# A held opening in another order: chunk 3's scores ahead of chunk 2's y, the first weight loaded one place later, step 0's out-products ahead of chunk 4's y

## The chip, the cores and the metric

The kernel runs on one core of one Trainium2 chip. The metric is the device time of one execution in microseconds (us); the median of several runs is compared. The engines are named as in the profile: PE is TensorE (matmuls), PEld its weight loads, DVE is VectorE, ACT is ScalarE, POOL is GpSimd and SP is SyncE, which issues nearly all DMAs.

## The reference

A decayed linear attention over 768 tokens (2 batches, 8 heads of 64), then an MLP with a GELU-like gate, then an RMS-normed SwiGLU MLP, all in float32; the weights of the MLPs come as float64.

```python
for t in range(S):                       # attention
    state = gamma * state + outer(k[t], v[t])
    y[t] = scale * q[t] @ state
x = y.reshape(B * S, H * D)              # 1536 tokens x 512
h = x @ w_in                             # 512 x 2048
x = (h * sigmoid(1.702 * h)) @ w_out     # 2048 x 512
xn = x / sqrt(mean(x * x) + 1e-6) * rms_g
g = xn @ w_gate                          # 512 x 1536
out = (g * sigmoid(g) * (xn @ w_val)) @ w_out2
```

## The kernel before

**Tiling.** The attention goes by chunks of 128 tokens, six for each batch, with a state carried from chunk to chunk. The MLPs work on token tiles of 512: chunks 0 to 3 make the first tile. Float32 products are made as three products of a high and a low part (`product`, and `in_proj` for the first MLP's in-products): the high part is a copy in a shorter form that ScalarE makes, the low part is the remainder that VectorE makes from it (`halves`).

**A chunk of attention** has these parts. `score_products` (L287): sixteen matmuls in the trace, written to two PSUM tiles. `masks` (L301): two VectorE products with the decay mask. `inter` (L318): the first part of y, from the state so far and the decayed q (`prep_q`, GpSimd, L249). `intra` (L331): the second part of y, from the masked scores and v. `x_high` (ScalarE, L352) and `x_low` (VectorE, L358): y's two parts, which are the first MLP's input. `update_products` (L375): the new state's addend u, from v and the decayed k (`prep_k`, GpSimd, L256, or for chunk 4 `prep_k_by_head`, eight ScalarE pieces, L268). `decay` (ScalarE, four pieces, L383) and `add_update` (VectorE, L391): the state.

**A weight** comes as 64-bit words of 512 KB a half (`load_next`, SP, L143) and is converted in five steps (`convert`): two ScalarE copies (L174, L175), a shift (L176), an add (L177) and a sign step (L183) on VectorE. For step f of the first MLP, half 0 is the in-weight, split by `split_in` (`wih` on ScalarE, `wil` on VectorE, both in `halves`, L411 and L412), half 1 the out-weight, split by `split_out`. The weights are loaded and converted in the order in 0, in 1, out 0, in 2, out 1, in 3 and so on. Four staging buffers hold the loaded words, so a load waits for an earlier conversion.

**A step f of the first MLP** is `mlp1_in` (in-products h, L429, twelve matmuls), `mlp1_act` (activation g on ScalarE, L451, its high part gh, L444, its low part gl on VectorE, L445) and `mlp1_out` (out-products, twelve matmuls, L406 to L408, into four PSUM tiles acc that collect over all 16 steps).

**What sets the order.** In the opening (up to `ends = in_order(opening)`) each of PE, VectorE, ScalarE and GpSimd keeps the order in which the code is written: `in_order` ties every instruction to the one before it on its engine. An engine works through its list in order, so one that waits holds all behind it. From there on a scheduler places the instructions, tied to the opening's last ones for the first steps (`f < HELD`). SP's queue is one list of DMA issues, in order too.

Of the kernel before, what the change touches and what calls it, by code (L numbers as in the profile page):

```python
# [8 lines left out]
F32 = mybir.dt.float32  # L9
# [42 lines left out]
def tile_retention_mlp_swiglu(  # L52
# [30 lines left out]
    ps_a = pool("ps_a", 4, space=PSUM)  # L83
# [42 lines left out]
    raw = {}  # L126
# [11 lines left out]
    def load_next():  # L138
        n = count["loaded"]
        if n < len(queue):  # L140
            kind, i, half = queue[n]
            t = st_p.tile([128, 512], U64, tag="st", name=f"{kind}{i}{half}_64")
            nc.sync.dma_start(out=t, in_=sources[kind][i][:, half * 512:half * 512 + 512])  # L143
            words[queue[n]] = t
            count["loaded"] += 1
# [54 lines left out]

    parts = {}

    def split_in(f):
        if f < F1:
            t = parts["wi", f] = [wa_p.tile([128, 512], F32R, tag=f"wa{s}", name=f"wi{s}{f}") for s in "hl"]
            halves(*t, raw["w1", f][:, 0:512].bitcast(F32))

    def both(t):
        return t[:, 0:512], t[:, 512:1024]
# [23 lines left out]
    def load_qk(c):  # L233
        p, tag = (wr_p, "wr") if c < CPB else (ld_p, "ld")
        t = p.tile([128, 2, NP, C], F32, tag=tag, name=f"qk{c}")
        nc.sync.dma_start(out=t.rearrange("p a n c -> p (a n c)"), in_=qk[c])
        ld["qk", c] = t

    def load_kv(c):
        p, tag = (wr_p, "wr") if c < CPB else (ld_p, "ld")  # L240
        t = p.tile([128, 2, H, D], F32, tag=tag, name=f"kv{c}")
        nc.sync.dma_start(out=t.rearrange("p a h d -> p (a h d)"), in_=kv[c])
        ld["kv", c] = t
# [163 lines left out]
        nc.tensor.matmul(out=out, lhsT=ah, rhs=bl, start=False, stop=False)  # L407
        nc.tensor.matmul(out=out, lhsT=al, rhs=bh, start=False, stop=last)  # L408

    def halves(hi, lo, src):  # L410
        nc.scalar.activation(out=hi, in_=src, func=ACTF.Copy)  # L411
        nc.vector.tensor_tensor(out=lo, in0=src, in1=hi.bitcast(F32), op=ALU.subtract)  # L412

    def two_parts(f):
# [410 lines left out]
    load_kv(1)  # L825
    load_qk(2)
    load_kv(2)
    load_next()
    load_qk(3)
    load_kv(3)  # L830
    for _ in range(3):
        load_next()
# [31 lines left out]
    score_products(2, ps_a)  # L864
    masks(2)
    inter(2, ps_h)
    r = convert_next(split=True)
    for step in r[:3]:
        step()
    update_products(2, ps_t)  # L870
    add_update(2)
    r[3]()
    intra(2)
    prep(3)
    x_high(2)
    score_products(3, ps_a)
    masks(3)
    x_low(2)
    r[4]()
    decay(3)  # L880
    load_next()
    r = convert_next(split=True)
    r[0]()
    r[2]()
    inter(3, ps_h)
    intra(3)
    update_products(3, ps_t)
    x_high(3)
    x_low(3)
    split_in(0)  # L890
    r[1]()
    r[3]()
    r[4]()
    load_next()
    add_update(3)
    r = convert_next(split=True)
    r[0]()
    r[1]()
    split_in(1)
    ps = mlp1_in(0)  # L900
    score_products(CPB, ps_t)
    r[2]()
    r[3]()
    ready = of(mybir.EngineType.DVE)[-1]
    masks(CPB)
    prep_q(CPB)
    tc.add_manual_dep(of(mybir.EngineType.Pool)[-1], ready.name, WAIT, reason="order of issue")
    r[4]()
    load_next()
    mlp1_act(0, ps)  # L910
    prep_k_by_head(CPB)
    split_out(0)
    ends = in_order(opening)
    opened = len(nc.cur_bb.bb.instructions)

# [34 lines left out]
    for f in range(1, F1):  # L950
        begun = len(nc.cur_bb.bb.instructions)
        rest = []
        while count["converted"] < min(2 * f + 4, 2 * F1):
            if f == JOIN and count["converted"] == 2 * f + 3:
                rest = convert_next(split=True)
                for step in rest[:2]:
                    step()
            else:
                convert_next()
        split_out(f)  # L960
        if not rest:
            split_in(f + 2)
        if f == F1 - 3:
            start_set(0)
        if f == F1 - 2:
            phase.close()
            later["wb"] = side(ctx, "wb", 3)
            later["gs"] = side(ctx, "gs", 3)
            mops = deque(m_tasks())
            start_set(1)  # L970
            some(mops, 1)
            some(sets[0], 1)
        if f == F1 - 1:
            some(mops, 3)
            early = [nc.cur_bb.bb.instructions[-1]]
            some(sets[0], 1)
            early.append(nc.cur_bb.bb.instructions[-1])
            some(mops, 1)
            some(sets[0], 2)
            y_high = nc.cur_bb.bb.instructions[-2]  # L980
        ps = mlp1_in(f)
        next_of(att)
        if rest:
            masked = of(mybir.EngineType.DVE)[-1]
            for step in rest[2:]:
                step()
                after(of(mybir.EngineType.DVE)[-1], masked)
            load_next()
            split_in(f + 2)
        mlp1_act(f, ps)  # L990
        if f == F1 - 1:
            for i in early:
                after(nc.cur_bb.bb.instructions[-1], i)
        if f < HELD:
            for x in nc.cur_bb.bb.instructions[begun:]:
                if x.engine in ends:
                    after(x, ends[x.engine])
        mlp1_out("wo", 0, f - 1)
        if f in (4, 9):
            next_of(att)  # L1000
    assert not att
# [11 lines left out]
    order = []  # L1013
# [307 lines left out]
```

## Time and profile before

| | |
|---|---|
| median of 3 runs | 586.10 us (585.87 to 586.41) |
| profiled execution | 586.26 us |
| its span in the trace | 584.1 us |
| PE busy | 577.6 us (99%) |
| DVE busy | 452.6 us (77%) |
| ACT busy | 364.8 us (62%) |
| POOL busy | 25.0 us (4%) |

A row of the page's engine part gives an engine's busy time, its share of the span and its instructions. A busy PE is not PE at its peak, since matmuls overlap and their ends are modelled; the starts in the view by time tell more. In that view a row is a run of equal instructions: start and duration in us, engine, line, operation, what is written from what, the tile's shape, the count, and in brackets the idle time of the engine before it with the one that ended it. A float32 matmul of the attention shows as two PE instructions.

### The profile page before, as it was taken

What the parts mean: (1) busy time and instruction counts of PE and PEld (TensorE: products, weight loads), DVE (VectorE), ACT (ScalarE), POOL (GpSimd) and SP (SyncE); (2) the same over time, 40 slices, a digit from 0 to 9 for tenths busy, and PEclk for the clock granted to TensorE, in tenths of its full rate; (3) what the DMA queues carried; (4) which work ended last, traced back from release to release, by engine and by line L of the source; (5) the groups of instructions that cost most, each with busy time, mean ns of one, the idle gap of its engine ahead of it and who ended that gap; (6) DMA issues with size and microseconds to landing.
All of it is one profiled execution on the core that took longest, in us unless ns stands there. A gap on an engine that the chain in (4) does not pass through costs nothing.

```text
span 584.1 us, 9262 instructions
## 1 busy us (share of the span) xinstructions
PE 577.6 (99%) x3264; PEld 481.8 (82%) x3264; DVE 452.6 (77%) x808; ACT 364.8 (62%) x696; POOL 25.0 (4%) x26
## 2 busy tenths in 40 slices
PE   8999999999999999999999999999999999999997
PEld 6787887888788888878888888888989889988885
DVE  2899988878999888467998998888868676644552
ACT  2778777667777887466647875666555446534441
POOL 4210122100000000000000000000000000000000
PEclk9999999999999999999999999999999999999999
DMA  8989999887369899878754236666514486560512
GB/s 329 405 265 379 388 333 361 280 279 241 139 233 339 295 337 341 306 245 323 281 161 174 108 121 209 194 229 219 165 59 141 145 288 231 189 223 8 176 41 72
DMA packets 47854, 135.09 MB, mean 231 GB/s; under 512 B 5568, under 2 KB 5824, under 8 KB 47808
## 3 DMA queue, kind: packets, MB, share of 16 engines
q1 hardware_dynamic: 47376, 134.37, 66.2%
q8 instruction: 25, 0.41, 0.3%
q10 hardware_dynamic: 432, 0.14, 0.1%
q14 instruction: 21, 0.17, 0.1%
HBM read 98.84 MB, written 35.65 MB: 230 GB/s over the span
## 4 chain that ended last, share of the span: by engine, by line
PE 98%; DMA 1%; ACT 0%; DVE 0%; issue 0%; DVEq 0%
PE acc L406 8%; PE h L429 8%; PE acc L407 7%; PE acc L408 7%; PE o L407 6%; PE o L408 6%; PE o L406 6%; PE sc L287 2%; PE y L331 2%; PE y L318 2%; PE m7a L735 1%; PE v0a L735 1%; PE m0a L735 1%; PE g10a L735 1%; PE g8a L735 1%; PE g6a L735 1%
## 5 line engine op out<-in xcount | busy, mean ns | idle before, releaser
L407 PE MATMUL o<-w,gh 128*128 128x512 f32 x144 | 56.2, 391 | 0.0
L406 PE MATMUL o<-w,gh 128*128 128x512 f32 x144 | 56.2, 390 | 0.0
L408 PE MATMUL o<-w,gl 128*128 128x512 f32 x144 | 56.1, 390 | 0.0
L177 DVE CUSTOM_DVE_ANT_0 qw<-qw,uw 128x1024 uint16<-128x1024 uint16 x68 | 46.6, 686 | 3.2 <-ACT uw L175 0.7
L174 ACT ACTIVATE qw<-w 128x512 f32<-128x512 f32 x68 | 45.2, 665 | 2.0 <-DMA w<-in_w 2.0
L175 ACT ACTIVATE uw<-w 128x512 uint32<-128x512 uint32 x68 | 45.3, 666 | 0.0
L176 DVE TENSOR_SCALAR qw<-qw 128x512 uint32<-128x512 uint32 x68 | 30.4, 449 | 9.3 <-ACT qw L174 9.3
L412 DVE TENSOR_TENSOR gl<-gw,gh 128x512 fp32r<-128x512 f32 x24 | 16.6, 691 | 27.1 <-ACT gh L411 27.0
L411 ACT ACTIVATE gh<-gw 128x512 fp32r<-128x512 f32 x24 | 15.1, 631 | 28.6 <-PE o L407 22.2
L408 PEld LDWEIGHTS o<-w,gl 128*128 128x128 f32 x144 | 27.0, 188 | 5.6
L407 PEld LDWEIGHTS o<-w,gh 128*128 128x128 f32 x144 | 27.1, 188 | 4.6
L406 PEld LDWEIGHTS o<-w,gh 128*128 128x128 f32 x144 | 27.1, 188 | 4.6
L406 PE MATMUL acc<-gh,wo 128*128 128x512 f32 x64 | 25.9, 413 | 0.0
L429 PE MATMUL h<-xt0h,wih 128*128 128x512 f32 x64 | 24.4, 397 | 0.7 <-ACT wih L411 0.7
L408 PE MATMUL acc<-gh,wo 128*128 128x512 f32 x64 | 25.1, 392 | 0.0
L407 PE MATMUL acc<-gl,wo 128*128 128x512 f32 x64 | 25.0, 391 | 0.0
L407 PE MATMUL acc<-gl,wowp 128*128 128x512 f32 x64 | 25.0, 390 | 0.0
L408 PE MATMUL acc<-gh,wowp 128*128 128x512 f32 x64 | 24.9, 390 | 0.0
L406 PE MATMUL acc<-gh,wowq 128*128 128x512 f32 x64 | 24.9, 389 | 0.0
L408 PE MATMUL acc<-gh,wowq 128*128 128x512 f32 x64 | 24.9, 389 | 0.0
L407 PE MATMUL acc<-gl,wowq 128*128 128x512 f32 x64 | 24.9, 389 | 0.0
L183 DVE SCALAR_TENSOR_TENSOR qw<-w,qw 128x512 uint32<-128x512 uint32 x36 | 24.7, 686 | 0.2
(1513 smaller groups left out, 1692.7 us busy)
## 6 DMA issues: line engine op xcount, KB each, us to landing
w<-in_w SPq DMA_DIRECT2D x68, 512.0 KB, 6.0
qk<-in_qk SPq DMA_DIRECT2D x12, 512.0 KB, 7.5
kv<-in_kv SPq DMA_DIRECT2D x12, 512.0 KB, 8.3
gmd<-gm SPq DMA_DIRECT2D x16, 256.0 KB, 4.6
gwm<-gmd SPq DMA_DIRECT2D x16, 256.0 KB, 5.5
g1d<-gs SPq DMA_DIRECT2D x12, 256.0 KB, 2.1
g2d<-gl SPq DMA_DIRECT2D x12, 256.0 KB, 2.8
gw<-g1d SPq DMA_DIRECT2D x12, 256.0 KB, 3.6
```

The lines of the kernel that those rows point to most:

```text
L174: lambda: nc.scalar.activation(out=q, in_=high.bitcast(F32), func=ACTF.Copy, scale=2.0 ** -112),
L175: lambda: nc.scalar.activation(out=t, in_=low, func=ACTF.Copy, scale=2.0 ** -29),
L176: lambda: nc.vector.tensor_scalar(out=m, in0=m, scalar1=3, scalar2=None, op0=ALU.logical_shift_left),
L177: lambda: nc.vector.tensor_tensor(out=m, in0=m, in1=t, op=ALU.add),
L183: nc.vector.scalar_tensor_tensor(out=dst, in0=high, scalar=0x80000000, in1=m, op0=ALU.bitwise_and, op1=ALU.bitwise_or)
L406: nc.tensor.matmul(out=out, lhsT=ah, rhs=bh, start=first, stop=False)
L407: nc.tensor.matmul(out=out, lhsT=ah, rhs=bl, start=False, stop=False)
L408: nc.tensor.matmul(out=out, lhsT=al, rhs=bh, start=False, stop=last)
L411: nc.scalar.activation(out=hi, in_=src, func=ACTF.Copy)
L412: nc.vector.tensor_tensor(out=lo, in0=src, in1=hi.bitcast(F32), op=ALU.subtract)
L429: nc.tensor.matmul(out=ps, lhsT=w[a][:, k * 128:(k + 1) * 128], rhs=x[b][:, k, :], start=o == order[0], stop=o == order[-1])
L735: nc.tensor.matmul(out=bank, lhsT=u, rhs=v, start=first and k == 0 and x == 0, stop=k == 1 and x == 2, skip_group_check=True,)
```

## The change

Only the opening's written order changes, and the first places of the weight loads. What moves:

- on SP, chunk 3's qk is loaded before the first weight, which it followed;
- chunk 3's `score_products`, `masks` and `prep_q` come before chunk 2's `intra`; the first weight's conversion comes behind chunk 3's masks, all five steps together;
- `split_in` and `halves` take a piece of code that is run between the high and the low part: for step 0 that is x_high and x_low of chunk 3, so these come behind `wih` and ahead of `wil`;
- `decay(3)` comes behind the second weight's ScalarE steps, `update_products(3)` behind step 0's in-products, `prep_k(3)` waits for the first weight's sign step;
- the in-products of step 1, its activation and the out-products of step 0 are now written in the opening, and are left out of the loop's first turn; chunk 4's scores come behind the in-products of step 1, chunk 4's y (which the loop writes) behind the out-products of step 0.

On VectorE, from chunk 3's masks (a3) on. In the names a and sc are masked and raw scores with their chunk's number, S_sb the state, u its addend, qw and uw a weight on its way through the conversion, w10 the converted in-weight of step 0, w11 that of step 1, xt0l the low part of the MLP's input, y2 and y3 the chunks' y. Before:

```order
L176 TENSOR_SCALAR qw100_281<-qw100_281 128x512
L391 TENSOR_TENSOR S_sb0_99<-u2_286,S_sb0_99 128x256
L177 ISA qw100_281<-qw100_281,uw100_282 128x1024
L301 TENSOR_TENSOR a3_0_320<-sc3_0_310,dm_sb_97 128x512
L301 TENSOR_TENSOR a3_1_322<-sc3_1_311,dm_sb_97 128x512
L358 TENSOR_TENSOR xt0l_194<-y2_271,xt0h_193 128x4x128
L183 SCALAR_TENSOR_TENSOR w10_280<-w100_64_133,qw100_281 128x512
L176 TENSOR_SCALAR qw110_337<-qw110_337 128x512
L358 TENSOR_TENSOR xt0l_194<-y3_341,xt0h_193 128x4x128
L412 TENSOR_TENSOR wil0_370<-w10_280,wih0_369 128x512
```

After:

```order
L391 TENSOR_TENSOR S_sb0_99<-u2_280,S_sb0_99 128x256
L301 TENSOR_TENSOR a3_0_310<-sc3_0_292,dm_sb_97 128x512
L301 TENSOR_TENSOR a3_1_312<-sc3_1_293,dm_sb_97 128x512
L176 TENSOR_SCALAR qw100_315<-qw100_315 128x512
L177 ISA qw100_315<-qw100_315,uw100_316 128x1024
L183 SCALAR_TENSOR_TENSOR w10_314<-w100_64_135,qw100_315 128x512
L358 TENSOR_TENSOR xt0l_194<-y2_271,xt0h_193 128x4x128
L358 TENSOR_TENSOR xt0l_194<-y3_332,xt0h_193 128x4x128
L414 TENSOR_TENSOR wil0_350<-w10_314,wih0_349 128x512
L176 TENSOR_SCALAR qw110_369<-qw110_369 128x512
```

The two masks of chunk 3 stood behind two of the first weight's three steps and stand ahead of all three; both x_low rows stand behind the first weight's sign step.

On ScalarE, around step 0's out-weight (wo0) and step 2's in-weight (wih2). g and gh are a step's activation and its high part, kd4 the decayed k of chunk 4; w120, w111 and w130 are the fourth to sixth weight loaded. Before:

```order
L451 ACTIVATE g0_422<-h0_388 128x512
L444 ACTIVATE gh0_424<-g0_422 128x512
L268 ACTIVATE kd4_428<-kv4_148,sm_sb_101 128x64 x8
L411 ACTIVATE wo0_437<-w10_280 128x512
L174 ACTIVATE qw120_443<-w120_64_143 128x512
L175 ACTIVATE uw120_444<-w120_64_143 128x512
L174 ACTIVATE qw111_458<-w111_64_334 128x512
L175 ACTIVATE uw111_459<-w111_64_334 128x512
L352 ACTIVATE xr1_517<-y4_500 128x4x128
L383 ACTIVATE S_sb0_99<-S_sb1_100,sm_sb_101 128x64
L411 ACTIVATE wih2_454<-w12_442 128x512
```

After:

```order
L411 ACTIVATE wo0_435<-w10_314 128x512
L453 ACTIVATE g1_446<-h1_396 128x512
L446 ACTIVATE gh1_448<-g1_446 128x512
L268 ACTIVATE kd4_452<-kv4_148,sm_sb_101 128x64 x8
L174 ACTIVATE qw120_478<-w120_64_143 128x512
L175 ACTIVATE uw120_479<-w120_64_143 128x512
L174 ACTIVATE qw111_493<-w111_64_330 128x512
L175 ACTIVATE uw111_494<-w111_64_330 128x512
L174 ACTIVATE qw130_503<-w130_64_390 128x512
L175 ACTIVATE uw130_504<-w130_64_390 128x512
L411 ACTIVATE wih2_489<-w12_477 128x512
```

The decayed k of chunk 4 and the out-weight have changed places, step 1's activation has come in between, and three conversions (six rows) stand between kd4 and wih2 where there were two, a y copy and a piece of decay.

The diff:

```diff
@@ -200,10 +200,10 @@
 
     parts = {}
 
-    def split_in(f):
+    def split_in(f, between=None):
         if f < F1:
             t = parts["wi", f] = [wa_p.tile([128, 512], F32R, tag=f"wa{s}", name=f"wi{s}{f}") for s in "hl"]
-            halves(*t, raw["w1", f][:, 0:512].bitcast(F32))
+            halves(*t, raw["w1", f][:, 0:512].bitcast(F32), between)
 
     def both(t):
         return t[:, 0:512], t[:, 512:1024]
@@ -407,8 +407,10 @@
         nc.tensor.matmul(out=out, lhsT=ah, rhs=bl, start=False, stop=False)
         nc.tensor.matmul(out=out, lhsT=al, rhs=bh, start=False, stop=last)
 
-    def halves(hi, lo, src):
+    def halves(hi, lo, src, between=None):
         nc.scalar.activation(out=hi, in_=src, func=ACTF.Copy)
+        if between:
+            between()
         nc.vector.tensor_tensor(out=lo, in0=src, in1=hi.bitcast(F32), op=ALU.subtract)
 
     def two_parts(f):
@@ -825,8 +827,8 @@
     load_kv(1)
     load_qk(2)
     load_kv(2)
+    load_qk(3)
     load_next()
-    load_qk(3)
     load_kv(3)
     for _ in range(3):
         load_next()
@@ -864,52 +866,50 @@
     score_products(2, ps_a)
     masks(2)
     inter(2, ps_h)
-    r = convert_next(split=True)
-    for step in r[:3]:
-        step()
     update_products(2, ps_t)
     add_update(2)
-    r[3]()
+    prep_q(3)
+    score_products(3, ps_a)
     intra(2)
-    prep(3)
+    masks(3)
+    r = convert_next(split=True)
+    for step in r[:4]:
+        step()
     x_high(2)
-    score_products(3, ps_a)
-    masks(3)
+    r[4]()
+    ready = of(mybir.EngineType.DVE)[-1]
     x_low(2)
-    r[4]()
-    decay(3)
+    prep_k(3)
+    tc.add_manual_dep(of(mybir.EngineType.Pool)[-1], ready.name, WAIT, reason="order of issue")
     load_next()
-    r = convert_next(split=True)
-    r[0]()
-    r[2]()
     inter(3, ps_h)
     intra(3)
-    update_products(3, ps_t)
-    x_high(3)
-    x_low(3)
-    split_in(0)
-    r[1]()
-    r[3]()
-    r[4]()
-    load_next()
-    add_update(3)
+    split_in(0, lambda: (x_high(3), x_low(3)))
+    first_h = mlp1_in(0)
     r = convert_next(split=True)
     r[0]()
     r[1]()
+    decay(3)
+    for step in r[2:]:
+        step()
+    update_products(3, ps_t)
+    load_next()
     split_in(1)
-    ps = mlp1_in(0)
+    second_h = mlp1_in(1)
+    add_update(3)
+    mlp1_act(0, first_h)
+    for step in convert_next(split=True):
+        step()
+    load_next()
     score_products(CPB, ps_t)
-    r[2]()
-    r[3]()
+    split_out(0)
     ready = of(mybir.EngineType.DVE)[-1]
     masks(CPB)
     prep_q(CPB)
     tc.add_manual_dep(of(mybir.EngineType.Pool)[-1], ready.name, WAIT, reason="order of issue")
-    r[4]()
-    load_next()
-    mlp1_act(0, ps)
+    mlp1_act(1, second_h)
     prep_k_by_head(CPB)
-    split_out(0)
+    mlp1_out("wo", 0, 0)
     ends = in_order(opening)
     opened = len(nc.cur_bb.bb.instructions)
 
@@ -978,7 +978,8 @@
             some(mops, 1)
             some(sets[0], 2)
             y_high = nc.cur_bb.bb.instructions[-2]
-        ps = mlp1_in(f)
+        if f > 1:
+            ps = mlp1_in(f)
         next_of(att)
         if rest:
             masked = of(mybir.EngineType.DVE)[-1]
@@ -987,7 +988,8 @@
                 after(of(mybir.EngineType.DVE)[-1], masked)
             load_next()
             split_in(f + 2)
-        mlp1_act(f, ps)
+        if f > 1:
+            mlp1_act(f, ps)
         if f == F1 - 1:
             for i in early:
                 after(nc.cur_bb.bb.instructions[-1], i)
@@ -995,7 +997,8 @@
             for x in nc.cur_bb.bb.instructions[begun:]:
                 if x.engine in ends:
                     after(x, ends[x.engine])
-        mlp1_out("wo", 0, f - 1)
+        if f > 1:
+            mlp1_out("wo", 0, f - 1)
         if f in (4, 9):
             next_of(att)
     assert not att
```

## Rows read from the trace of the kernel before

**Rows 1.** The page: PE's busy line, and the granted clock in 40 slices.

```profile
PE 577.6 (99%) x3264; PEld 481.8 (82%) x3264; DVE 452.6 (77%) x808; ACT 364.8 (62%) x696; POOL 25.0 (4%) x26
...
PEclk9999999999999999999999999999999999999999
```

**Rows 2.** Waits of PE, whole span: waited for, us in total, times, longest.

```profile
PE h L429 <- ACT wih L411: 0.7, 1, 0.7
```

**Rows 3.** PE by time, 0 to 60 us: start, duration, row as explained above.

```profile
4.19 2.08 PE L287 MATMUL sc<-qk 64*128 64x128 f32 x16 [0.69 <-DMA qk<-in_qk]
...
16.52 0.69 PE L375 MATMUL u<-kv,kd 128*64 128x64 f32 x16
17.03 1.05 PE L331 MATMUL y<-a,kv 128*64 128x128 f32 x16
18.01 1.16 PE L287 MATMUL sc<-qk 64*128 64x128 f32 x16
19.10 1.09 PE L318 MATMUL y<-qd,S_sb 64*64 64x128 f32 x16
20.12 1.47 PE L331 MATMUL y<-a,kv 128*64 128x128 f32 x15
...
22.91 1.20 PE L429 MATMUL h<-xt0h,wih 128*128 128x512 f32 x4 [0.74 <-ACT wih L411]
...
25.85 1.16 PE L287 MATMUL sc<-qk 64*128 64x128 f32 x16
...
31.84 0.64 PE L375 MATMUL u<-kv,kd 128*64 128x64 f32 x16
32.40 0.50 PE L406 MATMUL acc<-gh,wo 128*128 128x512 f32 x1
...
35.26 0.39 PE L429 MATMUL h<-xt0h,wih 128*128 128x512 f32 x1
```

**Rows 4.** VectorE by time, 0 to 60 us.

```profile
19.27 1.29 DVE L301 TENSOR_TENSOR a<-sc,dm_sb 128x512 f32<-128x512 f32 x2 [0.98 <-PE sc L287]
20.48 0.68 DVE L358 TENSOR_TENSOR xt0l<-y,xt0h 128x512 fp32r<-128x512 f32 x1
...
22.37 0.69 DVE L358 TENSOR_TENSOR xt0l<-y,xt0h 128x512 fp32r<-128x512 f32 x1 [0.27 <-ACT xt0h L352]
22.98 0.68 DVE L412 TENSOR_TENSOR wil<-w,wih 128x512 fp32r<-128x512 f32 x1
23.57 0.69 DVE L177 CUSTOM_DVE_ANT_0 qw<-qw,uw 128x1024 uint16<-128x1024 uint16 x1
24.30 0.69 DVE L183 SCALAR_TENSOR_TENSOR w<-w,qw 128x512 uint32<-128x512 uint32 x1
...
26.30 0.42 DVE L176 TENSOR_SCALAR qw<-qw 128x512 uint32<-128x512 uint32 x1
```

**Rows 5.** ScalarE by time, 0 to 60 us.

```profile
21.74 0.60 ACT L352 ACTIVATE xt0h<-y 128x512 fp32r<-128x512 f32 x1 [1.40 <-PE y L331]
22.23 0.62 ACT L411 ACTIVATE wih<-w 128x512 fp32r<-128x512 f32 x1
22.75 0.66 ACT L175 ACTIVATE uw<-w 128x512 uint32<-128x512 uint32 x1
23.31 0.66 ACT L174 ACTIVATE qw<-w 128x512 f32<-128x512 f32 x1
...
25.02 0.63 ACT L411 ACTIVATE wih<-w 128x512 fp32r<-128x512 f32 x1 [0.49 <-DVE w L183]
26.02 0.60 ACT L451 ACTIVATE g<-h 128x512 f32<-128x512 f32 x1 [0.36 <-PE h L429]
26.64 0.63 ACT L444 ACTIVATE gh<-g 128x512 fp32r<-128x512 f32 x1
27.18 2.02 ACT L268 ACTIVATE kd<-kv,sm_sb 128x64 f32<-128x64 f32 x8
...
33.04 0.61 ACT L411 ACTIVATE wih<-w 128x512 fp32r<-128x512 f32 x1
```

## The prediction

> **What bounds the kernel now.** I read the page first: the TensorE is busy 577.6 of 584.1 us [rows 1]. Then I asked who it waits for: after the first score group there is one wait that the view names, 0.7 us before the first in-product (h0), for a weight's high part from the ScalarE [rows 2]. So the end is set by TensorE's own work, and by whatever holes stand in it: a hole at any place moves everything behind it. The only stretch with holes is the opening, and there the row-by-row view of the TensorE shows two [rows 3]: chunk 3's second y part (fifteen of its sixteen matmuls at 20.12) takes 1.47 us where the sixteen at 17.03 take 1.05, and h0 at 22.91 has waited 0.74. From 22.91 on it runs from group to group without a hole: h0 and chunk 4's scores until 26.9, u4 at 31.84, step 0's out-products at 32.40, h2 at 35.26. All that the change can win is those two holes, about 1.2 us.
>
> The second thing the reader should see is how the engines that feed it hand work on. ScalarE and VectorE each run their list in the order in which it is written. A ScalarE result is taken by VectorE 0.03 us after its end (x_high of chunk 3 ends at 21.74 + 0.60 = 22.34, x_low starts at 22.37), and back likewise (24.30 + 0.69 = 24.99, next 25.02) [rows 4, 5]. So the opening's feed can be added up by hand.
>
> **The change part by part.** Nothing is computed more or less; matmuls, conversions and loads are the same, in another order.
>
> *Loads.* Chunk 3's qk goes ahead of the first weight. Each is 512 KB, so they change places and nothing behind them moves. The first weight is not late for it: its ScalarE conversion stays behind chunk 2's decay, where it stands today, and its VectorE steps now start about 3 us later than that. I cost this at nothing.
>
> *Chunk 3's scores before chunk 2's y.* u2 stands at 16.52 as before; a u group takes 0.56 (31.84 to 32.40), so sc3 starts at 17.08 instead of 18.01 [rows 3]. The first mask follows a score group's start by 1.26 (18.01 to 19.27), the two masks hold VectorE 1.21 (19.27 to 20.48) [rows 3, 4]. The hole before chunk 3's y goes: masks are done at 19.6, before TensorE has gone through sc3 (1.09), chunk 2's y (0.98, 17.03 to 18.01) and chunk 3's first y part (1.02, 19.10 to 20.12), at 20.17. TensorE is through with chunk 3's y (0.98) at 21.15.
>
> *What the same edit costs.* VectorE's list now has both masks of chunk 3 ahead of all three steps of the first weight; before, two of the three stood ahead of them. From the rows: shift step (L176) 18.34 + 1.21 = 19.55; add step (L177) + 0.42 + 0.03 = 20.00; sign step (L183) + 0.73 (23.57 to 24.30) = 20.73; the weight's high part on ScalarE + 0.72 (24.30 to 25.02) = 21.45 [rows 4, 5]. And ScalarE's list now has that high part ahead of chunk 3's x_high, so x_high follows at + 0.52 (22.23 to 22.75) = 21.97 and ends at 22.57. h0 needs both, 0.06 after the later (22.23 + 0.62 to 22.91): 22.63. TensorE waits 1.5 us there. It then does h0 0.28 us earlier than before, but without u3, which took 0.56 ahead of h0 and now comes behind it: it is 0.28 us later.
>
> *h1, no longer behind chunk 4's scores.* The chain goes on without a pause: x_low 22.60, low part of the first weight + 0.61 = 23.21, L176 of the second weight + 0.59 = 23.80, L177 24.25, L183 24.98, its high part 25.70, so h1 at 25.70 + 0.68 = 26.38 [rows 4, 5]. TensorE is free at 22.63 + 2.94 (22.91 to 25.85) + 0.56 for u3 = 26.13: a wait of 0.25. Before, chunk 4's scores covered this.
>
> *Step 0's out-products ahead of chunk 4's y.* ScalarE: activation of h0 at 25.70 + 0.52 = 26.22, its high part + 0.62 (26.02 to 26.64) = 26.84, conversion of the third weight at 27.38 and 27.94 (0.54 and 0.56 apart: 26.64 to 27.18, 22.75 to 23.31). VectorE: activation's low part at 27.50, L176 28.10, L177 28.63 (it waits for the second conversion, 27.94 + 0.66), L183 29.36. High part of the out-weight on ScalarE 30.08, ends 30.70; its low part on VectorE 30.73 to 31.41 [rows 4, 5]. TensorE has h1 until 29.32 and chunk 4's scores until 30.41; the out-products start at 30.76 (wait 0.35), and the third one waits 0.14 more for the low part. They take 2.86 (32.40 to 35.26), so end at 33.76. Before, chunk 4's y and u4 (2.5 us) stood between and covered both waits. Then y and u4, 1.02 + 0.98 + 0.56: TensorE stands at h2 at 36.32, where it stood at 35.26 [rows 3]: 1.06 us lost so far.
>
> *h2.* This is the dearest term. Before, ScalarE made kd4 (eight pieces, 27.18, 2.02 us) before the out-weight's high part and had h2's weight high part out at 33.04, two us ahead of need [rows 5]. Now the list after the out-weight (30.08) runs: activation of h1 30.60, its high part 31.22, kd4 31.76, and then three conversions of two each, six instructions, before h2's high part. kd4 2.02 less the 0.10 by which one instruction overlaps the next = 33.68; six by 0.56 = 3.36: 37.04. h2 can start at 37.04 + 0.68 = 37.72, and its third matmul needs the low part: VectorE, with the sign step of another weight ahead of it, comes to it at about 38.0, done 38.7, a further 0.5. TensorE waits 1.4 + 0.5 = 1.9 us.
>
> *Sum.* 1.06 + 1.9 = 3.0 us later at the end of h2. Nothing behind gives it back, since TensorE has no hole behind [rows 2]; and since the feed behind h2 has the same work as before against a TensorE that is 3 us later, I add none either. Chunk 6's loads now stand ahead of weight loads on SP's queue, and kv waits for u4's end at 36.3, which holds the weight loads behind it; the first of those weights is for h4, two steps on, so I cost it at nothing, and at about 1 us if the ScalarE, waiting for it, were to hold step 1's activations too. GpSimd's kd3 and qd4 are made later (after L183 at 21.4, after 31.4); u3 at 25.6 and chunk 4's y at 33.8 still find them done.
>
> The profiled run took 586.26 us for a span of 584.1, the median is 586.10. 586.2 + 3.0 gives **589.2 us**. Bounds: without the low part's wait at h2 and with each of some twelve handoffs 0.03 shorter, + 2.1; with each 0.03 longer and 1 us for SP's queue, + 4.4.
>
> **The rivals.**
> 1. *The holes close (faster).* The two holes of [rows 3] go and nothing takes their place: 586.2 - 1.2 = 585.0. It is decided by h0's feed: with the first weight's VectorE steps done by 20.0, in the hole of VectorE ahead of chunk 3's masks, x_high would run at 21.2 as TensorE comes free. Against it: the list has L176 behind both masks.
> 2. *Only the opening pays.* The waits up to the out-products come, 1.06 us, but h2 does not wait, because ScalarE gets through its list faster than row by row: 587.3. It needs h2's high part 1.4 us sooner, that is two to three instructions fewer. Against it: pitches of 0.52 to 0.57 repeat in every row.
> 3. *The clock falls in the new waits.* The first score group, at the kernel's start, takes 2.08 us; the same group at 18.01 takes 1.16 [rows 3]: the lower level (1.2 GHz) against 2.4. The granted-clock line shows 9 in all slices [rows 1], so it does not tell the two apart; the durations do. If the wait at h2 brought that level back for h2 and the next out-products (2.8 + 2.86 us), they would take that much more: 589.2 + 5.7 = 594.9. Against it: after the wait of 0.74 at 22.91 h0's twelve matmuls take 2.94, the full level. For it: the new waits are twice as long.
> The Trainium skill has a rule for this (TensorE: Matmul & The Clock Gate, "HAM oscillation — how this bites in real kernels"): idle gaps between groups of matmuls make the clock go back to 1.2 GHz and each such gap is paid again. [...]
>
> **How the numbers follow.** Forecast (chain as added up) 0.78: inside it 588.3 to 590.6. Rival 1: 0.06. Rival 2: 0.11. Rival 3: 0.05. The range takes in the bounds of the forecast and rival 2: 587.2 to 590.6 holds about 0.8. A measurement of this kernel can tell 0.2% (1.2 us) from no change. Faster 0.06; same 0.12, which is rival 2 and the thinnest end of the forecast; slower 0.82.
>
> **What would show it.** In the changed trace: sc3 at 17.1; chunk 3's y without a hole at 20.2; h0 near 22.6 after a wait of 1.5 on ScalarE's x_high; h1 near 26.4; out-products near 30.8 and ahead of chunk 4's y; kd4 near 31.8 and h2 near 37.7 after about 1.4 us of waiting for ScalarE. Wrong would be: L176 of the first weight ahead of 19; h2's high part before 36; a TensorE hole behind h3; or groups of twice the length behind a wait.

## The result, and the profile after

| | before | after |
|---|---|---|
| median | 586.06 us (585.45 to 586.41, 6 runs) | 589.52 us (588.77 to 590.41, 6 runs) |
| ratio, 95% interval | | 1.0060 (1.0047 to 1.0073) |
| profiled execution | 586.26 us | 589.77 us |
| its span | 584.1 us | 586.9 us |

The change makes the kernel 3.5 us slower, 0.6%. On the chip of e1 to e4 below it took 589.05 us (6 runs) where before took 585.80 (30 runs), 3.25 us more; the ratio is 1.0048 (1.0032 to 1.0065). It takes in every execution and not the medians alone, and 3 of before's 30 took 589.1 to 591.7 us. e5 to e8 ran on another chip, e9 and e10 on one more; before took 585.81 (11 runs) and 586.01 us (9 runs) there. One execution of e1 (594.09 us) was in the chip's slow state and stands outside e1's ratio.

The page, and what PE waited for in the whole span (us in total, times, longest), which answer to [rows 1] and [rows 2]:

```profile
PE 577.8 (98%) x3264; PEld 480.5 (82%) x3264; DVE 454.3 (77%) x808; ACT 364.0 (62%) x696; POOL 25.1 (4%) x26
...
PEclk9999999999999999999999999999999999999999
```

```profile
PE h L431 <- ACT wih L411: 1.4, 2, 1.2
PE h L431 <- ACT xt0h L352: 1.3, 1, 1.3
...
PE acc L406 <- ACT wo L411: 0.3, 1, 0.3
PE h L431 <- DVE wil L414: 0.3, 1, 0.3
```

TensorE's work is the same (577.6 and 577.8 us). Where one wait of 0.7 us stood there are now five, 3.4 us in all by the rows below, and each is for a weight or for y's high part out of ScalarE or VectorE. PE by time (start, duration, row), which answers to [rows 3]:

```profile
15.54 0.69 PE L375 MATMUL u<-kv,kd 128*64 128x64 f32 x16
16.16 1.16 PE L287 MATMUL sc<-qk 64*128 64x128 f32 x16
...
19.30 1.09 PE L331 MATMUL y<-a,kv 128*64 128x128 f32 x16
21.74 1.20 PE L431 MATMUL h<-xt0h,wih 128*128 128x512 f32 x4 [1.35 <-ACT xt0h L352]
...
24.68 0.69 PE L375 MATMUL u<-kv,kd 128*64 128x64 f32 x16
25.62 1.19 PE L431 MATMUL h<-xt0h,wih 128*128 128x512 f32 x4 [0.25 <-ACT wih L411]
...
30.05 0.50 PE L406 MATMUL acc<-gh,wo 128*128 128x512 f32 x1 [0.32 <-ACT wo L411]
...
37.06 0.50 PE L431 MATMUL h<-xt0h,wih 128*128 128x512 f32 x1 [1.18 <-ACT wih L411]
...
38.05 0.50 PE L431 MATMUL h<-xt0h,wil 128*128 128x512 f32 x1 [0.26 <-DVE wil L414]
```

Chunk 3's y (19.30) now takes 1.09 without the hole of [rows 3]. Then come the waits: 1.35 ahead of h0, 0.25 ahead of h1, 0.32 ahead of the out-products, 1.18 and 0.26 in h2. Behind 38.05 none that the view names. The view counts a wait from the modelled end of the matmul ahead, which is late: by the starts, the 1.35 ahead of h0 is 1.46 (chunk 3's y at 19.30 takes 0.98 from start to start, as in [rows 3], and h0 starts at 21.74). So the named waits sum to less than TensorE loses.

The feed, VectorE and then ScalarE by time, which answer to [rows 4] and [rows 5]:

```profile
17.35 1.29 DVE L301 TENSOR_TENSOR a<-sc,dm_sb 128x512 f32<-128x512 f32 x2 [0.59 <-PE sc L287]
18.56 0.42 DVE L176 TENSOR_SCALAR qw<-qw 128x512 uint32<-128x512 uint32 x1
19.12 0.69 DVE L177 CUSTOM_DVE_ANT_0 qw<-qw,uw 128x1024 uint16<-128x1024 uint16 x1
19.85 0.69 DVE L183 SCALAR_TENSOR_TENSOR w<-w,qw 128x512 uint32<-128x512 uint32 x1
...
22.93 0.42 DVE L176 TENSOR_SCALAR qw<-qw 128x512 uint32<-128x512 uint32 x1
23.49 0.69 DVE L177 CUSTOM_DVE_ANT_0 qw<-qw,uw 128x1024 uint16<-128x1024 uint16 x1
```

```profile
20.57 0.63 ACT L411 ACTIVATE wih<-w 128x512 fp32r<-128x512 f32 x1 [1.58 <-DVE w L183]
21.11 0.58 ACT L352 ACTIVATE xt0h<-y 128x512 fp32r<-128x512 f32 x1
...
29.37 0.63 ACT L411 ACTIVATE wo<-w 128x512 fp32r<-128x512 f32 x1 [1.52 <-DVE w L183]
29.91 0.58 ACT L453 ACTIVATE g<-h 128x512 f32<-128x512 f32 x1
30.52 0.63 ACT L446 ACTIVATE gh<-g 128x512 fp32r<-128x512 f32 x1
31.05 2.01 ACT L268 ACTIVATE kd<-kv,sm_sb 128x64 f32<-128x64 f32 x8
...
36.39 0.61 ACT L411 ACTIVATE wih<-w 128x512 fp32r<-128x512 f32 x1
...
44.23 0.66 ACT L174 ACTIVATE qw<-w 128x512 f32<-128x512 f32 x1 [3.63 <-DMA w<-in_w]
```

Both masks (17.35) stand ahead of the first weight's shift step (18.56), and ScalarE has nothing to do for 1.58 us until its sign step is out. At 29.37 ScalarE has idled again, 1.52 us, and then has kd4 and six conversions to do before h2's weight at 36.39.

**Positions.** This execution reached u2, chunk 2's update group, at 15.54, the profiled one of before at 16.52. The stretch ahead of u2 is no measure of a kernel: executions with the very same opening reached it from 15.54 (this one) to 16.75 (e6 below). TensorE's clock rose earlier in this one: chunk 0's y takes 1.09 us at 7.93 here, and 1.98 at 8.17 in e6. So from here on positions are counted from the start of u2 in each trace, and the table gives them less those of before (us; each is the start of a group's first row, the last column the end of the last matmul; out is step 0's first out-product):

| | h0 | h1 | out | h2 | h3 | h6 | h12 | end |
|---|---|---|---|---|---|---|---|---|
| before, from u2 | 6.39 | 10.42 | 15.88 | 18.74 | 25.50 | 48.45 | 96.01 | 563.45 |
| after | -0.19 | -0.35 | -1.37 | +2.77 | +3.44 | +3.83 | +3.83 | +3.73 |
| e4, after again | -0.19 | -0.35 | -1.37 | +2.77 | +3.45 | +3.62 | +3.62 | +3.56 |
| e1, loads alone | +0.01 | +0.03 | +0.03 | +0.03 | +0.03 | +0.03 | +0.03 | -0.12 |
| e2, first half | +0.45 | +0.71 | +0.72 | +0.72 | +0.81 | +0.98 | +4.55 | +4.42 |
| e10, the same again | +0.45 | +0.72 | +0.72 | +0.72 | +0.83 | +0.83 | +0.83 | +0.72 |
| e3, second half | 0.00 | -1.18 | -1.79 | +2.36 | +3.04 | +3.03 | +3.03 | +2.91 |
| e5, kd4 first | -0.19 | -0.35 | -1.10 | +1.81 | +2.68 | +2.67 | +2.67 | +2.57 |
| e6, wih2 first | -0.19 | -0.35 | -1.38 | +2.07 | +3.75 | +3.86 | +3.87 | +3.78 |
| e7, two steps ahead of the masks | -0.84 | -1.01 | -2.03 | +2.13 | +2.81 | +2.81 | +2.81 | +3.54 |
| e8, scores alone | -0.41 | -0.41 | -0.41 | -0.41 | -0.41 | -0.41 | -0.41 | -0.35 |
| e9, the same again | -0.42 | -0.41 | -0.41 | -0.41 | -0.41 | -0.18 | +4.83 | +4.74 |

Groups that the change itself moves forward (h1, out) stand early in its rows without that being a gain; h2 is the first at which the work done is the same. Of what a row has lost by h3, at most 0.15 us has come back at its end.

### The profile page after: what moved, and what is told of

It is laid out like the page before. It is cut to its first block, busy times and chain, and to the rows that moved or that the text cites. A ratio compares the mean times of both kernels' runs of the same rounds, so it can differ in the third digit from the quotient of the medians.

```text
span 586.9 us, 9255 instructions
## 1 busy us (share of the span) xinstructions
PE 577.8 (98%) x3264; PEld 480.5 (82%) x3264; DVE 454.3 (77%) x808; ACT 364.0 (62%) x696; POOL 25.1 (4%) x26
## 4 chain that ended last, share of the span: by engine, by line
PE 94%; DVE 2%; ACT 2%; DMA 1%; issue 1%; SPq 0%; POOL 0%; DVEq 0%; POOLq 0%
PE acc L406 8%; PE acc L407 7%; PE acc L408 7%; PE h L431 7%; PE o L406 6%; PE o L407 6%; PE o L408 6%; PE sc L287 2%; PE y L331 1%; PE y L318 1%; DMA qd_sb<-in_qdec 1%; PE m7a L737 1%; PE v0a L737 1%; PE m0a L737 1%; PE m1a L737 1%; PE g10a L737 1%
## 5 line engine op out<-in xcount | busy, mean ns | idle before, releaser
L177 DVE CUSTOM_DVE_ANT_0 qw<-qw,uw 128x1024 uint16<-128x1024 uint16 x68 | 46.6, 685 | 2.5 <-ACT uw L175 0.7
L176 DVE TENSOR_SCALAR qw<-qw 128x512 uint32<-128x512 uint32 x68 | 28.8, 425 | 10.6 <-ACT qw L174 10.6
L183 DVE SCALAR_TENSOR_TENSOR qw<-w,qw 128x512 uint32<-128x512 uint32 x36 | 24.7, 685 | 0.2
```

The source lines that it names most:

```text
L176: lambda: nc.vector.tensor_scalar(out=m, in0=m, scalar1=3, scalar2=None, op0=ALU.logical_shift_left),
L177: lambda: nc.vector.tensor_tensor(out=m, in0=m, in1=t, op=ALU.add),
L183: nc.vector.scalar_tensor_tensor(out=dst, in0=high, scalar=0x80000000, in1=m, op0=ALU.bitwise_and, op1=ALU.bitwise_or)
```

## The experiments

The theory to be tested: the price is made in the lists of ScalarE and VectorE, mostly by the second half (out-products and h1 ahead of chunk 4's y, kd4 behind the out-weight), and once made it stays to the end. The rivals: the first half or the loads make it; or SP's queue.

**e1: the loads alone.** Before, with chunk 3's qk ahead of the first weight:

```diff
+    load_qk(3)
     load_next()
-    load_qk(3)
     load_kv(3)
```

> The kernel before with the loads alone changed: chunk 3's qk ahead of the first weight. Theory (the price lies in the order of ScalarE's and VectorE's lists): no change, 586.1 within 0.3 us; the first weight's two ScalarE copies still stand behind chunk 2's decay and do not start later. Rival (the first weight comes too late, the loads are to blame): its copies wait for its DMA, the shift step on VectorE goes from 18.3 to 19 or later, h0 follows, and the time rises by 0.5 us or more.

586.07 us over 12 runs, ratio 1.0008 (0.9992 to 1.0023): no change, and the table shows 0.03 us up to h12. The first weight did land later, at 16.16 us after the span's start and not 14.28, and ScalarE waited 0.75 us for it, which was not expected; h0 does not move for that, since the sign step waits its turn behind the masks in any case. The loads are not to blame.

**e2: the first half alone.** The loads, chunk 3's scores and masks ahead, all of the first weight behind the masks, its high part ahead of x_high(3); u3, chunk 4's scores and the out-products as before:

```diff
-    r = convert_next(split=True)
-    for step in r[:3]:
-        step()
...
+    prep_q(3)
+    score_products(3, ps_a)
     intra(2)
-    prep(3)
+    masks(3)
+    r = convert_next(split=True)
+    for step in r[:4]:
+        step()
     x_high(2)
...
     update_products(3, ps_t)
-    x_high(3)
-    x_low(3)
-    split_in(0)
+    split_in(0, lambda: (x_high(3), x_low(3)))
...
```

> The first half of the change alone: loads swapped, chunk 3's scores ahead of chunk 2's y, all of the first weight behind chunk 3's masks, its high part ahead of chunk 3's x_high. From h0 on the order of before: u3 ahead of h0, chunk 4's scores between h0 and h1, the out-products behind chunk 4's y. Theory: this half costs little, since chunk 4's scores and y stand again where they cover the feed: h0 some 0.3 to 0.5 us later than before (u3 now waits for GpSimd's decayed k, which is made behind the first weight's sign step), 0.4 to 1.1 us in all, 586.5 to 587.2. Rival 1 (the first half is the dear one): + 2.5 to + 3.5 us, 588.6 or more. Rival 2 (the holes of the opening were worth it): 585.0 to 585.7.

Its 12 executions fall into two groups, six from 585.8 to 587.5 and six from 590.1 to 591.3 us (median of all 588.79, ratio 1.0036, 1.0007 to 1.0064). That median lies where rival 1 had it, the six shorter ones around the theory's 586.5 to 587.2, so the trace has to decide. The opening is as expected: + 0.81 us at h3. The rest of the profiled execution's loss lies far behind it, as its waits show:

```profile
PE y L318 <- DVE a L301: 3.4, 2, 2.7
PE u L375 <- POOL kd L256: 1.4, 1, 1.4
```

The second line is the price in the opening (u3 ahead of h0 waits for the decayed k, which GpSimd makes behind the sign step). The first line is two waits for the masks of later chunks, near 84 and 99 us. This is a mishap that the theory had not foreseen; e8 to e10 follow it up. Rival 1, that the first half is the dear one, is out for the opening: it costs 0.8 us there.

**e3: the second half alone.** The opening of before up to u3, then the new order:

```diff
-    r = convert_next(split=True)
-    r[0]()
-    r[1]()
     split_in(1)
-    ps = mlp1_in(0)
+    first_h = mlp1_in(0)
+    second_h = mlp1_in(1)
+    mlp1_act(0, first_h)
+    for step in convert_next(split=True):
+        step()
+    load_next()
     score_products(CPB, ps_t)
...
+    split_out(0)
...
+    mlp1_act(1, second_h)
     prep_k_by_head(CPB)
-    split_out(0)
+    mlp1_out("wo", 0, 0)
...
```

> The second half of the change alone: the opening of before up to u3, then h0 and h1 in a row, chunk 4's scores, step 0's out-products ahead of chunk 4's y, step 1's activation ahead of chunk 4's decayed k on ScalarE. Theory: this half carries nearly all of the price: waits ahead of h1 and of the out-products, and more than 1 us ahead of h2 for the high part of its weight on ScalarE; + 2.4 to + 3.3 us, 588.5 to 589.4. Rival (the first half is the dear one, this one only fills in): less than + 1 us.

588.69 us, ratio 1.0037 (1.0022 to 1.0053), 2.9 us more than before, and + 3.04 at h3. Its rows for the out-products and for h2 (PE by time):

```profile
30.18 0.50 PE L406 MATMUL acc<-gh,wo 128*128 128x512 f32 x1 [0.77 <-ACT wo L411]
...
37.18 0.50 PE L429 MATMUL h<-xt0h,wih 128*128 128x512 f32 x1 [1.22 <-ACT wih L411]
```

The wait at h2 is that of after (1.18) without any of the first half. The second half alone makes 3.0 of the 3.4 us. The two halves sum to 3.85, not 3.44, so they share some 0.4 us. The out-products' wait is the likely place: 0.77 us in e3 and 0.32 in after, where TensorE comes later already; that it is the whole of it is not shown.

**e4: the changed kernel again.**

> The changed kernel again, beside the others on one chip. Theory: 589.5 within 0.5 us, h2 about 2.8 us later than before counted from u2, with waits of about 1.3 us ahead of h0 and 1.2 to 1.4 us ahead of h2. If e2 and e3 add up to this run's difference, the halves are independent; if e3 alone is as much, the first half costs nothing once the second is there, because its delay is taken up in the wait at h2.

589.05 us. Up to h3 its positions are those of after within 0.01 us. Neither of the two cases came out: the halves do not quite add up, and e3 alone is not as much, so about half of the first half's 0.8 us is taken up by the second. The difference between the two executions comes behind: after lost another 0.4 us from h3 to h6, this one 0.2.

**e5: kd4 ahead of the out-weight again**, the changed kernel otherwise:

```diff
+    prep_k_by_head(CPB)
     split_out(0)
...
     mlp1_act(1, second_h)
-    prep_k_by_head(CPB)
```

> The changed kernel with one step taken back: on ScalarE chunk 4's decayed k (kd4, eight pieces, 2 us) stands ahead of step 0's out-weight high part again, as before the change. Theory (h2 waits because kd4, step 1's activation and three conversions stand in one row between the out-weight and h2's weight): kd4 falls into ScalarE's wait of 1.5 us for the out-weight's sign step, so h2's weight is 1.0 to 1.5 us earlier, the waits at h2 shrink by as much, and the time is 1.0 to 1.5 us less than the changed kernel's, 587.5 to 588.1 against 585.8 of before. Rival (SP's queue holds the weight loads, or the sign step's feed on VectorE sets h2): the wait at h2 stays above 1 us and the time is the changed kernel's within 0.4 us.

588.51 us over 4 runs, ratio 1.0048 (1.0035 to 1.0061), above the 587.5 to 588.1 expected and 0.5 under e4's 589.05; the two intervals overlap, so the trace has to decide. h2's weight is 1.27 us earlier than in after, as expected, h2 starts 0.96 us earlier, just under it, and h3 0.76, which is less. ScalarE, and the third matmul of h2:

```profile
27.88 2.00 ACT L268 ACTIVATE kd<-kv,sm_sb 128x64 f32<-128x64 f32 x8
29.78 0.61 ACT L411 ACTIVATE wo<-w 128x512 fp32r<-128x512 f32 x1
...
35.24 0.63 ACT L411 ACTIVATE wih<-w 128x512 fp32r<-128x512 f32 x1 [0.29 <-DVE w L183]
```

```profile
37.40 0.50 PE L431 MATMUL h<-xt0h,wil 128*128 128x512 f32 x1 [0.46 <-DVE wil L414]
```

kd4 fills ScalarE's idle 1.52 us and pushes the out-weight back by 0.3. But now h2's weight waits for its own sign step (0.29), and the wait for its low part grows from 0.26 to 0.46: VectorE's list is the next limit. So about 0.8 us of the price was kd4's place, and the theory holds with VectorE as the one behind it.

**e6: step 2's in-weight held ahead of the later conversions**, the changed kernel otherwise (a tie of later ScalarE instructions to its high part).

> The changed kernel with step 2's in-weight high part held ahead of the later conversions on ScalarE, as soon as its sign step is done. Theory: its high part comes out up to 1.1 us earlier, but the low part on VectorE and the conversions behind it move back, so that h2 starts earlier and a part returns as a wait at chunk 5's scores or at the out-products behind: 0.4 to 1.1 us less than the changed kernel, 588.0 to 588.7. Rival (conversions ahead of it are not the cause): h2 where it was, time the same.

589.39 us over 4 runs, 1.0060 (1.0045 to 1.0075): nothing won. h2 is 0.70 us earlier than in after, as expected, and h3 is 0.31 later. The reason is not a wait. PE by time, chunk 5's scores:

```profile
40.76 1.16 PE L287 MATMUL sc<-qk 64*128 64x128 f32 x8
...
43.21 1.16 PE L287 MATMUL sc<-qk 64*128 64x128 f32 x8
```

In every other kernel here this group is one row of sixteen and takes 1.16 or 1.17; here the scheduler, given that tie, put its two halves at two places, and eight take 1.16 as well. In the whole group the matmuls start two by two, 0.01 us apart; a half alone has no partners. The edit moved more than it was meant to, so the time says nothing on ScalarE's order; only the start of h2 does.

**e7: two of the first weight's three VectorE steps ahead of chunk 3's masks again**, the changed kernel otherwise:

```diff
+    r = convert_next(split=True)
+    for step in r[:3]:
+        step()
     add_update(2)
+    r[3]()
...
     masks(3)
-    r = convert_next(split=True)
-    for step in r[:4]:
-        step()
```

> The changed kernel with the first weight's shift and add steps put ahead of chunk 3's masks on VectorE again, in the hole there; sign step behind the masks. This is the point from which the prediction's first rival decides. Theory: the wait of 1.3 us ahead of h0 shrinks by about 0.6 to 0.7 us (the sign step still follows the masks), and since the feed is one chain from there the whole stays 0.5 to 0.7 us earlier, to the end: 588.4. Rival (h2's wait is set by its own feed and takes up what is won at h0): h0 earlier but h2 where it was, the time within 0.2 us of the changed kernel's.

588.76 us over 4 runs, ratio 1.0055 (1.0042 to 1.0068). In the trace the gain is passed on whole: - 0.65 us against after at h0, - 0.64 at h2, - 0.63 at h3. So the rival, that h2's wait would take it up, is out, and the feed is one chain from the first mask to h2. VectorE:

```profile
17.71 0.68 DVE L177 CUSTOM_DVE_ANT_0 qw<-qw,uw 128x1024 uint16<-128x1024 uint16 x1
18.31 1.28 DVE L301 TENSOR_TENSOR a<-sc,dm_sb 128x512 f32<-128x512 f32 x2
19.51 0.68 DVE L183 SCALAR_TENSOR_TENSOR w<-w,qw 128x512 uint32<-128x512 uint32 x1
```

The sign step still stands behind the masks, 0.34 us earlier than in after by the clock of the trace and 0.79 by distance from u2 (15.99 there). The median is 0.3 us under e4's and not 0.6; in the profiled execution 0.7 us went again near 152 us, where TensorE waited 0.55 for a high part of the second MLP's input. Whether that comes with the edit, this one profile can't tell.

**e8: chunk 3's scores ahead, two steps of the first weight still ahead of the masks.** Before, with chunk 3's scores ahead of chunk 2's second y part; the first weight's high and low parts also come ahead of chunk 3's x_high and x_low, and decay(3) later:

```diff
-    intra(2)
     prep(3)
-    x_high(2)
     score_products(3, ps_a)
+    intra(2)
     masks(3)
-    x_low(2)
+    x_high(2)
     r[4]()
-    decay(3)
     load_next()
+    x_low(2)
+    split_in(0)
...
+    decay(3)
     add_update(3)
```

> The kernel before with chunk 3's scores alone put ahead of chunk 2's second y part, and the first weight's shift and add steps left ahead of the masks; the out-weight order of before, u3 ahead of h0, decay(3) later. Theory: the hole in chunk 3's y goes (0.4 us) and of the 0.7 us ahead of h0 a part: 0.5 to 0.9 us faster than before, 584.9 to 585.3, near the least this resolves. Rival (the masks one place earlier delay the weight and h0 waits longer): 585.8 or above; and if the feed far behind the opening is upset as in e2, 587 or more.

In the profiled execution (585.98 us) the theory's gain is there, though smaller than expected: 0.41 us from h0 to h12, 0.35 at the end. The other five took 589.0 to 592.8 (median of the six 590.85; ratio 1.0076, 1.0047 to 1.0105). None of these five was profiled; e9 shows one such execution of the same kernel. No version here beats before by its median.

**e9 and e10: e8 and e2 again**, to see where the executions part.

> The kernel of e8 again, to see where the 3 to 6 us lie that most of its executions took more than the profiled one (which had no wait behind h0 and ended 0.4 us early, counted from u2). Theory: as in e2's profile, GpSimd's decayed q and k of chunks 7 to 9 run beside VectorE's products there, which then take 1.5 to 1.8 us and not 0.7, the weight's sign step and the masks come late, and TensorE waits 1 to 3 us between 70 and 100 us; h0 to h3 stand 0.4 us early as in e8. Rival: the waits lie in the opening, between u2 and h3, where the masks' new place may be too tight; or there is no wait at all and groups of matmuls take twice as long (clock).

> The kernel of e2 again: its profiled execution stood 0.8 us behind before at h3 and 4.6 us behind at h10, half of its executions are 4 us shorter. Theory: the opening costs the same 0.8 us in each, and what differs are the two waits for chunk 8's and 9's masks near 83 and 96 us; in an execution without them the end stands at + 0.8 to + 1.0 us counted from u2. Rival: the opening itself differs.

e10's eight executions took 585.4 to 586.8 us five times, then 588.4, 590.4 and 591.6 (median 586.75; ratio 1.0032, 1.0001 to 1.0064); e9's two took 591.68 and 591.63. e10's profiled execution took 585.98 us and has no wait behind the opening: + 0.83 us from h3 to h12, where e2 had + 4.55. e9's took 591.68: 0.41 early up to h3 like e8, and 4.83 late at h12. So the opening is the same in both pairs and the loss is behind it, as expected. VectorE and GpSimd in e9 at the place, then VectorE at the same place in e8:

```profile
92.21 1.64 DVE L177 CUSTOM_DVE_ANT_0 qw<-qw,uw 128x1024 uint16<-128x1024 uint16 x1
93.77 1.53 DVE L412 TENSOR_TENSOR wo<-w,wo 128x512 fp32r<-128x512 f32 x1
...
97.20 1.28 DVE L301 TENSOR_TENSOR a<-sc,dm_sb 128x512 f32<-128x512 f32 x2
```

```profile
92.01 1.29 POOL L249 TENSOR_TENSOR qd<-qk,qd_sb 128x512 f32<-128x512 f32 x1 [11.99 <-DMA wo8d<-wo]
93.26 1.49 POOL L256 TENSOR_TENSOR kd<-kv,sm_sb 128x512 f32<-128x512 f32 x1
```

```profile
92.04 1.79 DVE L412 TENSOR_TENSOR wil<-w,wih 128x512 fp32r<-128x512 f32 x1 [0.70 <-ACT wih L411]
93.75 1.27 DVE L301 TENSOR_TENSOR a<-sc,dm_sb 128x512 f32<-128x512 f32 x2
```

In e9 two of VectorE's rows, 0.69 us elsewhere, take 1.64 and 1.53, each ending 0.55 us after the GpSimd row beside it (93.30, 94.75). In e8, with the feed three rows further on, one row is caught there, and the masks run at 93.75, not at 97.20. The pair parts much earlier, at the decayed q of chunk 5. GpSimd and VectorE in e9, then in e8:

```profile
38.86 1.31 POOL L249 TENSOR_TENSOR qd<-qk,qd_sb 128x512 f32<-128x512 f32 x1 [10.06 <-PE sc L287]
38.93 1.79 DVE L177 CUSTOM_DVE_ANT_0 qw<-qw,uw 128x1024 uint16<-128x1024 uint16 x1
```

```profile
39.06 3.45 POOL L249 TENSOR_TENSOR qd<-qk,qd_sb 128x512 f32<-128x512 f32 x1 [10.06 <-PE sc L287]
39.13 0.69 DVE L177 CUSTOM_DVE_ANT_0 qw<-qw,uw 128x1024 uint16<-128x1024 uint16 x1
```

Counted from u2 the two engines' rows start at the same places (22.47 and 22.54). In e9 VectorE's add step is held 1.1 us, in e8 GpSimd's product 2.2 us, and at the next add step e9's feed is 1.1 us behind e8's (25.19 and 24.08 from u2). In e9 a weight's ScalarE copy also waited 0.63 us for its DMA at 39.2, in e8 not at all. e2 and e10 part at 54 us: in e10 VectorE's row starts 0.09 us ahead of GpSimd's and keeps its length, in e2 it starts 0.25 behind and takes 1.34. What decides such a meeting was not tried.

## Why the prediction was right

It was right in direction, mechanism and size: 589.2 forecast, 589.52 measured, and 589.05 on the other chip. Counted from u2 it was short by 0.5 us at h3 (2.96 forecast, 3.44 measured) and by 0.6 to 0.8 at the end (+ 3.56 and + 3.73); that the medians come nearer is luck as far as the stretch ahead of u2 goes, which the forecast took as equal. By its own steps, with positions from u2 (forecast times less 16.52; after's less 15.54):

| step | forecast | after |
|---|---|---|
| chunk 3's scores | 0.56 | 0.62 |
| L176, L177, L183 of the first weight | 3.03, 3.48, 4.21 | 3.02, 3.58, 4.31 |
| its high part, x_high(3) | 4.93, 5.45 | 5.03, 5.57 |
| h0 | 6.11 | 6.20 |
| h1 | 9.86 | 10.08 |
| step 0's out-products | 14.24 | 14.51 |
| high part for h2 | 20.52 | 20.85 |
| h2 | 21.20 | 21.52 |

- **Bound.** TensorE's work and the holes in it: yes. The waits of the view sum to 3.4 us against one of 0.7, and no row of the table gives back more than 0.15 us of a loss.
- **Loads.** Costed at nothing, and right (e1). But the reason held by less than the text says: the first weight landed at 15.55 in after, at 17.20 in e4 and at 17.53 in e5. In e5 ScalarE's second copy ended at 18.89, 0.35 us ahead of the add step at 19.24; a landing much later would have cost time.
- **First half.** Its hole closed as forecast, and its wait came as forecast: 1.35 ahead of h0 in the view, 1.46 by the starts (forecast 1.5), since chunk 3's masks stand ahead of the shift step. e7 puts two steps back and gets 0.65 us.
- **h1 and the out-products.** Waits 0.25 and 0.32 where 0.25 and 0.35 stood.
- **h2, the dearest term.** Forecast 1.4 + 0.5 = 1.9 us. Measured 1.18 and 0.26 in the view, but h2 has lost 2.77 at its start and another 0.67 by h3, so 3.44 in all where 2.96 was forecast.
- **What was mis-sized.** Two small terms. In after L177 follows L176 by 0.56 us at the first two weights, and the sum took 0.45 (0.42 + 0.03, its length and a hand-off): 0.11 at each, 0.22 of the 0.32 by which h2 is late. The trace of before has both figures, 0.55 at 34.77 to 35.32 and 0.45 at 26.30 to 26.75. In the second VectorE had already waited for a ScalarE result later than the weight's second copy, in the first it had not; that this makes the difference is read from the order of the rows, not tried. The other term: the first matmul of a run, behind a wait or an attention group, is followed 0.33 us later and not 0.23 (37.06 to 37.39 and 38.05 to 38.38 in after, 32.40 to 32.73 in before). In h2 this happens twice, 0.2 us, and the low part itself holds the third matmul 0.4 us by the starts, where 0.5 was forecast: together nearly the 0.67.
- **Nothing behind.** It was 0.4 us in after and 0.2 in e4 between h3 and h6. A weight's load, costed at nothing with 1 us as the bound, did hold ScalarE for 3.63 us up to 44.23 (the same wait was 0.53 us in the kernel before), and TensorE lost 0.2 us from h3 to h4 in after and none in e4. Between the first weight's copies and h2 ScalarE waited for no load, and e5 moves h2 without touching SP's queue, so the queue did not set h2.
- **Rival 1, the holes close.** Refuted as argued: the first weight's steps are behind the masks. e8 shows what closing a hole would give when they are not: 0.41 us, not 1.2.
- **Rival 2, only the opening pays.** Refuted: ScalarE's list runs at the pitches added up, kd4 at 31.05 and h2's high part at 36.39.
- **Rival 3, the clock falls.** Refuted: behind the waits of 1.35 and 1.18 the groups keep their length (h0's first four 1.20, as in [rows 3]) and the granted clock stays at 1.00, the upper of its two levels (2.4 GHz). e9 shows what it would look like. PE by time behind its wait of 3.33, and the granted clock in the stretch (us, busy and count, clock, DMA share, GB/s):

```profile
98.03 1.77 PE L318 MATMUL y<-qd,S_sb 64*64 64x128 f32 x16 [3.33 <-DVE a L301]
99.73 1.97 PE L331 MATMUL y<-a,kv 128*64 128x128 f32 x16
```

```profile
98.00:102.00 4.00, 3.97 (x46) 0.57 0.84 257
```

Two groups that take 1.09 each at the upper level take 1.77 and 1.97, and 1.5 us more go on top of the wait; from 98.5 to 101.5 us the granted clock is 0.50, the lower level (1.2 GHz). In e2 the wait of 2.70 us ahead of the same group was followed by groups of 1.09 at 1.00. The Trainium skill (TensorE: Matmul & The Clock Gate, "HAM oscillation — how this bites in real kernels") describes a kernel whose clock falls back in every gap between its groups; e9's row agrees. The gaps of that example are longer than any that this change makes, so it is no case for this rival.

## What to carry to other kernels

When one engine runs without holes, a reorder that puts its consumer group ahead of independent work also takes away the cover of the feed; add up the feeding engines' lists row by row, hand-off by hand-off, before the move. A result that was two microseconds early because something else stood ahead of it is the first thing to look for, and the engine's idle time ahead of it is where the displaced work (here kd4) should go. An edit that gains a fraction of a microsecond in an opening can still tip a tight feed elsewhere, so look at the spread of the executions and not at one profile.

## What the runs showed of the hardware

- A VectorE row that starts behind a GpSimd product, both on SBUF operands, does not slow down by a share: where it was held, a row of 0.69 us ended 0.55 us after the GpSimd row (1.64 and 1.53 in e9), wherever in that row it began. Elsewhere VectorE's row keeps its length and GpSimd's is the longer one (1.50 in e10 at 53.79, 0.09 behind VectorE's, 1.04 alone; 3.45 in e8 at 39.06, 1.29 alone). The masks, whose scores come from PSUM, keep theirs beside GpSimd (two in 1.27 at 93.75 in e8). The Trainium skill (SBUF — State Buffer, "SBUF: two separate sides") describes the port pair of the two as an exclusive lock that the first to start holds for the whole instruction, and these rows agree.
- The programs of e2 and e8 each ran in two ways, in the pairs profiled 4 and 5 us apart at h12, with the same positions up to h3; in the longer ones the feed had fallen behind and met GpSimd at other rows. Before has longer executions too, 3 of 30 on one chip (589.1 to 591.7 us); none of them was profiled.
- Chunk 5's score products of 64 rows run two by two: sixteen in 1.16 us, and eight alone also in 1.16 (e6).
- The stretch up to u2 varied by 1.2 us between executions of kernels with the same opening, more than some of the effects studied here; where TensorE's clock rose later (chunk 0's y at 1.98 us in e6, 1.09 in after), u2 came later.
